# The last state-row blocks by half products, and four products in one bank

## The chip, the cores and the metric

The kernel runs on one core of a Trainium2 chip. The engines that the text speaks of are TensorE (PE; its weight loads are PEld), VectorE (DVE), ScalarE (ACT), GpSimd (POOL) and SyncE (SP), whose queue issues most of the DMAs. A time is the device time of one execution, in microseconds, and lower is better. The kernel before took 211.48, 212.24 and 214.16 us in three runs, median 212.24.

## The reference

Eight batches of attention between 512 tokens and 32 state rows, in both directions and in 8 heads of 64, are followed by a gated layer of width 1536. The 512 token rows and the 32 state rows of a batch go through the same layer.

```python
B, H, S, Ns, D = (8, 8, 512, 32, 64)
scores = scale * np.matmul(x, state.transpose(0, 1, 3, 2))
a = np.exp(scores - max);  a /= a.sum(-1)             # 512 x 32 in each head
xread = np.matmul(a, state)
scores2 = scale * np.matmul(state, x.transpose(0, 1, 3, 2))
a2 = softmax(scores2)
sread = np.matmul(a2, x)
attn_out = np.concatenate([xread, sread], axis=2)
x = attn_out.transpose(0, 2, 1, 3).reshape(B * S, H * D)   # 4352 rows of 512
gate = 1.0 / (1.0 + np.exp(-(x @ w_gate)))                 # 512 -> 1536
val = x @ w_val
return (gate * val @ w_out)                                # 1536 -> 512
```

## The kernel before, in words

**Token rows.** Since xread is a @ state, gate and value of a batch's token rows are a @ (state @ W). For each batch the kernel first forms SW = state @ W (32-row matmuls, `sw_mm`, line 286, and `sw_pair`, line 293, gate and value side by side), and then, for each of the twelve 128-wide blocks f of the 1536 columns, a gate half and a value half (`gv_half`, line 355): two matmuls of 512 columns each. ACT takes the tanh of the gate half (`gv_th`, line 364), DVE multiplies it with the value half into `glu` (`gv_glu`, line 369).

**Output product by seven half products.** glu @ w_out is cut in 2 x 2 blocks (two halves of the tokens; even and odd blocks f; two halves of the output columns) and done with seven products in the place of eight. The left operands are blocks of glu or sums of them (`s_sum`, line 414), the right ones blocks of w_out or sums of them. `w_mm(b, k, c)` (line 434) issues product k for one quarter of the tokens, six matmuls of 256 columns; "5a" in the table `order` is product 5, c = 0. Products that share a key add up in one PSUM bank. On the way the sums are read: V1 is product 1, U2 is 1 + 6, U4 is U2 + 5, and the four output blocks are V1 + 2, U2 + 5 + 3, U4 + 7 and U2 + 7 + 4. `w_keep` (ACT, line 439) copies a bank to SBUF, `w_add` (DVE, line 445) adds a bank to a kept tile, `w_out` (ACT, line 442) copies a bank to the output tile.

**Which products share a bank.** For the last two batches' outputs the table `CHAIN` holds: 1, 6, 5 and 3 follow each other in bank OU. For the others it is `KEY`: 1 and 6 share OU, then 5 and 3 start anew in OU, and DVE forms U4 and the last block by adding the kept U2.

**The order of the work** is written out by hand: each engine gets its instructions in the order in which the Python code names them, and works through them in that order. The main loop is `step(b, f)`, b = 2 to 7 and f = 0 to 11. A step of batch b does block f of gate and value of b, the products of `order[f]` for batch o = b - 1, and pieces of the preparation of batch nb = b + 1: two visits of state @ W (at f = 0 and f = 6, `sw_six`, three pairs of banks each), whose banks `sw_cp` (line 329, on ACT) copies out over the following steps, the scores (f = 1, 2) with their sums and reciprocals, and at f = 6 `rd_mm`, `rd_fin` (DVE, lines 273 and 275) and `rd_dma` (line 278): the state rows sread, normalised and transposed by a DMA on SP's queue into XS. SP's queue has the transposes of a, of XS and of x (lines 248, 278, 140) one behind the other. At f = 6 POOL also begins to cast the x of batch nb + 1 (lines 116 and 251).

**Banks.** There are eight, each with one tile at a time: G0 and G1 take gate and value halves, OU the products above, S0, S1, AT and the two of `X(b)` the rest. A tile is written only when every reader of the one before it in its bank is done.

**State rows.** The 256 state rows of all batches go through the layer at the end, as a ninth batch B. ACT reorders XS for this (line 1056), two columns at f = 9 and two at f = 10 of step 6. Blocks f = 0 to 7 of gate and value are computed by two groups of half products (`g_mm`, line 531, 128 x 128; g = 0 and 1, four blocks f each), woven into step(7, f) by the tables `g_main` and `g_side`. Their sums of weights (`g_wsum`, DVE, line 507) are spread over earlier steps by `g_early`. Like the products above, a group has a V1, U2 and U4 that ACT copies out (`g_keep`, line 540), DVE adds to (`g_add`, line 544), ACT takes the tanh of (`g_th`, lines 549 and 552) and DVE multiplies (`g_glu`, line 561). Blocks 8 to 11 are done directly after the loop by `last` (line 358, four matmuls of 256 columns for gate and for value). Then the output product of batch 7's tokens (`w_mm`, `p_mm`) and of the state rows (`q_mm`, line 571) ends the kernel.

## Time and profile before

| what | us |
|---|---|
| median of 3 runs (lowest, highest) | 212.24 (211.48, 214.16) |
| the profiled execution | 212.11 |
| its span, first to last instruction | 210.3 |
| TensorE busy | 202.2 |
| DVE busy | 168.5 |
| ACT busy | 135.0 |
| POOL busy | 79.4 |

The first 50 us of the span are loads and batches 0 and 1; steps of batch 2 to 7 run from 53 to 189, the tail from 189.3 on. Line numbers are those of the kernel before. In the views of the timeline a row gives the start, the time from the start to the end of the last of its instructions, the engine, the line, what is written and read, and in brackets how long the engine had been idle and what ended that. The recorded ends of matmuls are modelled, so in the chain of waits the time of a row is the time until the next one goes on.

### The profile page before, as it was taken

How to read it: one execution, taken by the hardware profiler on the slowest of the kernel's cores; microseconds unless marked ns; L12 is line 12 of the kernel's file. 1: busy time of each engine (PE TensorE's matmuls, PEld its weight loads, DVE VectorE, ACT ScalarE, POOL GpSimd, SP SyncE). 2: the span in 40 equal slices, each digit the busy share in tenths (PEclk: the TensorE clock that was granted, in tenths of full speed). 3: DMA queues.
4: the chain of work that ended last, by engine and by line, in shares of the span. 5: the costliest groups of instructions: out<-in, count | busy, mean ns of one | idle time of the engine just before them, and what ended most of it. 6: DMA issues, size and time to landing. Idle time of an engine off the chain costs nothing.

```text
span 210.3 us, 5452 instructions
## 1 busy us (share of the span) xinstructions
PE 202.2 (96%) x2137; PEld 132.1 (63%) x2137; DVE 168.5 (80%) x325; ACT 135.0 (64%) x254; POOL 79.4 (38%) x104
## 2 busy tenths in 40 slices
...
GB/s 198 178 192 192 213 288 189 120 203 52 78 208 343 131 100 64 311 118 136 298 95 67 155 101 16 44 102 202 12 47 0 203 2 3 0 97 100 7 151 148
DMA packets 40921, 27.15 MB, mean 129 GB/s; under 512 B 23616, under 2 KB 38720, under 8 KB 40896
## 3 DMA queue, kind: packets, MB, share of 16 engines
...
q10 hardware_dynamic: 432, 0.33, 0.5%
...
q14 instruction: 9, 0.07, 0.1%
...
## 4 chain that ended last, share of the span: by engine, by line
PE 91%; DMA 4%; POOL 2%; issue 1%; DVE 0%; POOLq 0%
PE gvp L355 30%; PE outp L434 29%; PE gvp L343 10%; DMA wgv<-in_moe_w_val_dram 4%; PE outp L454 4%; PE swp L286 4%; PE gvs L531 3%; PE outp L571 2%; PE swp L293 2%; PE gvp L358 2%; PE Sp L147 1%; PE outp L479 1%; POOL wgv L104 1%; PE rdp L262 1%; POOL xf L100 1%
## 5 line engine op out<-in xcount | busy, mean ns | idle before, releaser
L369 DVE SCALAR_TENSOR_TENSOR glu<-th,gvp 128x512 bf16<-128x512 f32 x96 | 64.9, 682 | 25.1 <-PE gvp L355 12.4
L364 ACT ACTIVATE th<-gvp 128x512 f32<-128x512 f32 (+1 forms) x100 | 59.1, 593 | 39.4 <-PE gvp L355 32.4
L355 PE MATMUL gvp<-aT,SW 128*128 128x512 bf16 x288 | 77.4, 379 | 0.0
L329 ACT CAST SW<-swp 128x512 bf16<-128x512 f32 x83 | 46.6, 591 | 9.5 <-PE swp L286 8.3
L434 PEld LDWEIGHTS <-Sm 128*128 128x128 bf16 x324 | 31.4, 98 | 11.0
L355 PEld LDWEIGHTS <-SW 128*128 128x128 bf16 x288 | 26.7, 98 | 17.0 <-issue 2.8
L200 POOL CAST Eb<-E 128x256 bf16<-128x256 f32 x32 | 13.7, 467 | 51.9 <-ACT E L167 51.9
L434 PE MATMUL outp<-tw,Sm 128*128 128x256 bf16 x240 | 31.6, 273 | 0.0
L434 PEld LDWEIGHTS <-glu 128*128 128x128 bf16 x240 | 23.3, 98 | 9.2
L434 PE MATMUL outp<-wo,glu 128*128 128x256 bf16 x168 | 22.7, 273 | 0.0
L343 PE MATMUL gvp<-aT,SW 128*128 128x512 bf16 x96 | 22.6, 379 | 0.0
L596 POOL DMA_DIRECT2D out_dram<-res x1 | 0.6, 612 | 50.4 <-ACT res L442 50.4
L227 POOL TENSOR_TENSOR ab<-E,ri 128x512 bf16<-128x512 f32 x13 | 14.3, 1101 | 10.9 <-DVE ri L210 6.3
L414 DVE TENSOR_TENSOR Sm<-glu 128x768 bf16<-128x768 bf16 x30 | 16.7, 558 | 0.0
L343 PEld LDWEIGHTS <-SW 128*128 128x128 bf16 x96 | 8.6, 98 | 10.5 <-issue 1.6
L445 DVE SCALAR_TENSOR_TENSOR res<-outp,U 128x512 f32<-128x512 f32 x20 | 13.6, 684 | 0.9 <-PE outp L454 0.9
L116 POOL CAST xb<-xf 128x1024 bf16<-128x1024 f32 x12 | 13.2, 1126 | 1.1 <-DMA xf<-in_x_dram 1.1
L167 ACT ACTIVATE E<-Sp 128x512 f32<-128x512 f32 x14 | 8.4, 598 | 7.1 <-PE Sp L147 5.7
L434 PE MATMUL outp<-wo,Sm 128*128 128x256 bf16 x84 | 11.3, 273 | 0.0
L251 POOL CAST xs<-xf 128x1024 bf16<-128x1024 f32 x10 | 10.2, 1043 | 0.0
L434 PE MATMUL outp<-tw,glu 128*128 128x256 bf16 x72 | 9.8, 273 | 0.0
L329 DVE CAST SW<-swp 128x512 bf16<-128x512 f32 x13 | 8.7, 684 | 1.2 <-PE swp L293 1.0
...
## 6 DMA issues: line engine op xcount, KB each, us to landing
...
```

The lines of the kernel that those rows point to most:

```text
L116: cp(xbs[b].rearrange("p c h d -> p h c d")[:, lo:lo + n], (xhs if b in xhs else xfs)[b][:, lo:lo + n])
L200: nc.gpsimd.tensor_copy(Ebs[b][:, c], E1s[b][:, c])
L227: (nc.gpsimd if eng is pool else nc.vector).tensor_tensor(half(b, i, abs_), e1, ri.unsqueeze(len(ri.shape)).to_broadcast(e1.shape), ALU.mult)
L251: pool(xs.rearrange("p c h d -> p h c d")[:, lo:lo + n, :, :D], xfs[b][:, lo:lo + n])
L329: cp(*sw_left.pop((b, lo, w, e)))
L343: nc.tensor.matmul(ps, SWs[b][:, g, w, fs], aTs[b][:, :, g], start=(g == 0), stop=(g == 1))
L355: nc.tensor.matmul(ps, SWs[b][:, g, w, fs], aTs[b][:, :, g], start=(g == 0), stop=(g == 1))
L364: nc.scalar.activation(th, held["gv", b, f][0], AF.Tanh, scale=0.5)
L369: nc.vector.scalar_tensor_tensor(glus[b][:, f], held["th", b, f], 1.0, held["gv", b, f][1], ALU.add, ALU.mult)
L414: eng.tensor_tensor(S_(b, t)[:, i], a, c, op)
L434: nc.tensor.matmul(wps[key][:, c], lhs[:, i, c * 128:(c + 1) * 128], rhs[:, i], start=(first and c == 0 and i == 0), stop=(i == NF // 2 - ...
L445: nc.vector.scalar_tensor_tensor(to, wps[key], 0.5, held["w", name], ALU.mult, ALU.add)
```

## The change

There are three edits. First, blocks 8 to 11 of the state rows become a third group, g = 2, of half products in banks S0, G1 and G0; `last` and its line 358 are gone, the weight sums of all groups move to other steps, with those of the third group in steps 6 and 7, and ACT's reorder of XS moves to f = 8 and 9 of step 6 (columns 0 and 1) and f = 0 of step 7 (columns 2 and 3). Second, `CHAIN` holds for every batch: 1, 6, 5 and 3 add up in OU from f = 0 to f = 10, ACT copies U4 out at f = 6 and the finished block at f = 10. For that 5b moves from f = 7 to f = 6 and 7a from f = 8 to f = 7. Third, the second visit of state @ W (f = 6) takes both gate/value banks in the place of one of them and OU, product 5a stands between this visit and the gate half, and which of G0 and G1 takes the gate changes with the batch and no longer at f = 6.

```diff
-    KEY = {1: 1, 6: 1, 2: 2, 5: 5, 3: 5, 7: 7, 4: 7}
     CHAIN = {1: 1, 6: 1, 5: 1, 3: 1, 2: 2, 7: 7, 4: 7}
 
     def w_mm(b, k, c):
 
         lhs, rhs = prod(b, k)
-        key = (CHAIN if b >= B - 2 else KEY)[k]
+        key = CHAIN[k]
         first = k == key
         if first and c == 0:
-            place = OU if key in (1, 5) else X(b)[key == 2]
...
@@ -523,7 +527,7 @@
         rhs = g_x(*{1: (0, 0), 2: (1, 0), 3: (1, 1)}[k]) if k < 4 else held["xt"][:, {4: 3, 5: 0, 6: 1, 7: 2}[k]]
         key = CHAIN[k]
         if k == key:
-            place = ((AT, S0, S0), (S1, AT, AT))[g][(1, 2, 7).index(k)]
+            place = ((AT, S0, S0), (S1, AT, AT), (S0, G1, G0))[g][(1, 2, 7).index(k)]
...
-    order = {0: "1a", 1: "1b", 2: "2a", 3: "2b", 4: "6a", 5: "6b", 6: "5a", 7: "5b", 8: "7a7b", 9: "3a", 10: "3b4a", 11: "4b"}
+    order = {0: "1a", 1: "1b", 2: "2a", 3: "2b", 4: "6a", 5: "6b", 6: "5a5b", 7: "7a", 8: "7b", 9: "3a", 10: "3b4a", 11: "4b"}
...
-    g_side = {0: ((g_xsum, 1), (s_sum, B - 2, 0, 1, nc.vector)),
+              8: ((1, 7),), 9: ((1, 5),), 10: ((1, 3),), 11: ((1, 4), (2, 1))}
+    g_side = {0: ((xs_order, 2), (xs_order, 3), (g_xsum, 1), (s_sum, B - 2, 0, 1, nc.vector)),
...
-              11: ((g_add, 1, 7, "U2"),)}
-
-    def sw_six(b, v):
+              11: ((g_add, 1, 7, "U2"), (g_keep, 2, "V1"))}
+
+    def sw_six(b, v, pair):
 
         if b not in SWs:
             SWs[b] = fp.tile((128, 2, 2, dff), BF, name="SW", bufs=2)
         lo = 768 * v
         x, y = X(b)
-        for k, places in enumerate((((x, G1), (S0, y), (OU, S1)) if v else ((OU, G0), (x, AT), (S0, S1)))):
...
@@ -970,16 +976,18 @@
 
         nb, o = (b + 1 if b + 1 < B else None), b - 1
         v, late = f // 6, 1 if b == 2 else 0
+        gb = ((G1, G0), (G0, G1))[b % 2 if nb else 0]
         if nb and f in (0, 6):
             if v:
                 rd_mm(nb, AT)
-            sw_six(nb, v)
+            sw_six(nb, v, gb)
             sw_cp(nb, v, 0, 1, act)
             sw_cp(nb, v, 2 * v, 0, act)
         todo = order[f]
-        gb = (G1, G0) if nb and not v else (G0, G1)
-
-        at = {0: 0, 6: 0, 10: 2, 11: 0}.get(f, len(todo)) if nb is not None else len(todo)
+        if nb and f == 6:
+            w_mm(o, 5, 0)
+            todo = todo[2:]
+        at = {0: 0, 10: 2, 11: 0}.get(f, len(todo)) if nb else len(todo)
...
         if f == 5 and nb:
             s_sum(o, 3, 1, nc.vector)
-        if f == 7:
-            if b == B - 1:
-                w_keep("U4", 1)
-            else:
-                held["w", "U4"] = fp.tile((128, 2, 256), FP, name="U4", bufs=1)
-                w_add(5, "U2", held["w", "U4"])
+        if f == 6:
+            w_keep("U4", 1)
...
         if f == 10:
-            if b == B - 1:
-                w_out(1, w_res(o, 0)[:, :, hi_])
-            else:
-                w_add(5, "U2", w_res(o, 0)[:, :, hi_])
+            w_out(1, w_res(o, 0)[:, :, hi_])
...
-        if b == B - 2 and f in (9, 10):
-            if f == 9:
-                held["XS"] = xp.tile((128, 4, B * Ns), BF, name="xb", padded_shape=(128, 4, H * D))
-            for j in (2 * f - 18, 2 * f - 17):
-                act(held["XS"][:, j].rearrange("p (n b) -> p n b", b=B), XS[:, :, j].rearrange("p b n -> p n b"))
+        if b == B - 2 and f in (8, 9):
+            xs_order(f - 8)
```

The tail, where `last(8)` to `last(11)` stood:

```diff
-    def last(f, *mid):
-        gv_half(B, f, 0, G0)
-        gv_th(B, f)
-        for k, c in mid:
-            w_mm(o, k, c)
-        gv_half(B, f, 1, (G1, S0)[f % 2])
-
-    last(8, (1, 0))
+    w_mm(o, 1, 0)
+    g_mm(2, 2)
     g_th(1, "U2")
-    gv_glu(B, 8)
     s_sum(o, 0, 1, nc.vector)
-    last(9, (1, 1), (2, 0))
+    g_add(2, 2, "V1")
+    g_mm(2, 6)
+    g_keep(2, "U2")
+    w_mm(o, 1, 1)
     w_keep("V1", 1)
-    gv_glu(B, 9)
+    g_th(2, "V1")
+    g_glu(1, "U2")
     s_sum(o, 1, 1, nc.vector)
-    g_glu(1, "U2")
-    last(10, (2, 1), (6, 0))
-    gv_glu(B, 10)
+    g_mm(2, 7)
+    g_mm(2, 5)
+    g_keep(2, "U4")
+    g_glu(2, "V1")
+    w_mm(o, 2, 0)
+    g_add(2, 7, "U4")
+    g_th(2, "U4")
+    w_mm(o, 2, 1)
     w_add(2, "V1", w_res(o, 0)[:, :, lo_])
     s_sum(o, 2, 1, nc.vector)
-    last(11, (6, 1))
+    g_mm(2, 3)
+    g_th(2, None)
+    g_glu(2, "U4")
...
+    w_mm(o, 6, 1)
     w_keep("U2", 1)
...
+    g_mm(2, 4)
+    g_add(2, 7, "U2")
+    g_th(2, "U2")
     p_mm(7, 0)
+    s_sum(o, 3, 0, nc.vector)
+    g_glu(2, "U2")
+    w_mm(o, 5, 0)
```

TensorE at step(6, 6), the first matmul of the visit's third pair and what follows, before (names: swp is the visit's bank, gvp a gate or value half, outp a bank of products):

```order
L293 LDWEIGHTS sTc_99
L293 MATMUL swp_2899<-wgv_101,sTc_99 32x512 [waits Activation_49]
...
L355 LDWEIGHTS SW_2280
L355 MATMUL gvp_2911<-aT_2545,SW_2280 128x512 [waits DVE_49]
...
L355 MATMUL gvp_2916<-aT_2545,SW_2280 128x512 [waits Activation_49]
...
L434 LDWEIGHTS Sm_104
L434 MATMUL outp_2919<-tw_103,Sm_104 128x256 [waits Activation_49]
```

And in the changed kernel:

```order
L293 LDWEIGHTS sTc_99
L293 MATMUL swp_2896<-wgv_101,sTc_99 32x512 [waits DVE_49]
...
L433 LDWEIGHTS Sm_104
L433 MATMUL outp_2705<-tw_103,Sm_104 128x256
...
L355 MATMUL gvp_2914<-aT_2550,SW_2278 128x512 [waits Activation_49]
...
L433 MATMUL outp_2705<-tw_103,Sm_104 128x256
...
L355 MATMUL gvp_2925<-aT_2550,SW_2278 128x512 [waits Activation_49]
```

The third pair's first matmul waits for DVE and no longer for ACT; 5a stands ahead of the gate half, and 5b ahead of the value half.

ACT from the tanh of f = 8 to that of f = 10 in step 6, before (th is a tanh, SW a cast of a visit's bank, COPY the reorder of XS):

```order
L364 ACTIVATE th_2961<-gvp_2958 128x512 [waits DVE_49,PE_49]
L329 CAST SW_2667<-swp_2900 128x2x256
L364 ACTIVATE th_2987<-gvp_2984 128x512 [waits DVE_49,PE_49]
L329 CAST SW_2667<-swp_2889 128x512
L1056 COPY xb_3001<-XS_105 128x256 [waits DMAHW4_49,DMAHW3_49,DMAHW5_49,DMAHW2_49,DMAHW6_49,DMAHW1_49,DMAHW7_49,DMAHW0_49,Pool_49]
L1056 COPY xb_3001<-XS_105 128x256
L364 ACTIVATE th_3007<-gvp_3004 128x512 [waits DVE_49,PE_49]
L1056 COPY xb_3001<-XS_105 128x256 x2
```

And in the changed kernel, where the last row is the copy of the finished block:

```order
L364 ACTIVATE th_2965<-gvp_2962 128x512 [waits DVE_49,PE_49]
L329 CAST SW_2664<-swp_2897 128x2x256
L511 COPY xb_2980<-XS_105 128x256 [waits DMAHW4_49,DMAHW5_49,DMAHW3_49,DMAHW6_49,DMAHW1_49,DMAHW7_49,DMAHW0_49,Pool_49]
L364 ACTIVATE th_2986<-gvp_2983 128x512 [waits DVE_49,PE_49]
L329 CAST SW_2664<-swp_2886 128x512
L511 COPY xb_2980<-XS_105 128x256
L364 ACTIVATE th_3004<-gvp_3001 128x512 [waits DVE_49,PE_49]
L441 ACTIVATE res_2822<-outp_2705 128x2x256 [waits PE_49]
```

The first copy, with its wait for the transposes, now stands ahead of the tanh of f = 9.

ACT in the tail, from the tanh of f = 11 of batch 7, before (E1 and xT hold the groups' V1, U2 and U4, gvs is a group's bank, V1 is the kept product of batch 7):

```order
L364 ACTIVATE th_3397<-gvp_3394 128x512 [waits PE_49,Activation_49]
L364 ACTIVATE th_3429<-gvp_3424 128x256 [waits DVE_49,PE_49]
L552 ACTIVATE E1_3236<-E1_3236 128x256 [waits DVE_49]
L364 ACTIVATE th_3451<-gvp_3446 128x256 [waits PE_49,Activation_49]
L439 ACTIVATE V1_3471<-outp_3431 128x512 [waits PE_49]
L364 ACTIVATE th_3481<-gvp_3476 128x256 [waits PE_49,Activation_49]
```

And in the changed kernel:

```order
L364 ACTIVATE th_3397<-gvp_3394 128x512 [waits PE_49,Activation_49]
L544 ACTIVATE E1_3427<-gvs_3407 128x512 [waits PE_49]
L556 ACTIVATE E1_3234<-E1_3234 128x256 [waits DVE_49]
L544 ACTIVATE E1_3427<-gvs_3407 128x512 [waits PE_49]
L438 ACTIVATE V1_3469<-outp_3435 128x512 [waits PE_49]
L556 ACTIVATE E1_3427<-E1_3427 128x256 [waits DVE_49]
L544 ACTIVATE xT_3167<-gvs_3407 128x512 [waits PE_49]
L556 ACTIVATE xT_3167<-xT_3167 128x256 [waits DVE_49]
```

The four tanhs of `last` are gone; three copies of bank gvs_3407, each ahead of or behind a tanh that waits for DVE, have come.

More of the change, by code (lines that the diff above doesn't have):

```diff
@@ L427, in w_mm @@
         lhs, rhs = prod(b, k)
-        key = (CHAIN if b >= B - 2 else KEY)[k]
+        key = CHAIN[k]
         first = k == key
         if first and c == 0:
-            place = OU if key in (1, 5) else X(b)[key == 2]
+            place = OU if key == 1 else X(b)[key == 2]
             wps[key] = place[0].tile((128, 2, 256), FP, name="outp", tag=place[1])
@@ L507, in g_wsum, with xs_order @@
         nc.vector.tensor_tensor(d, a, c, op)
+    def xs_order(j):
+        if j == 0:
+            held["XS"] = xp.tile((128, 4, B * Ns), BF, name="xb", padded_shape=(128, 4, H * D))
+        act(held["XS"][:, j].rearrange("p (n b) -> p n b", b=B), XS[:, :, j].rearrange("p b n -> p n b"))
     def g_x(k, h):
@@ L538, in g_keep @@
             gk["U4"] = ap_.tile((128, 2, 2, 2, 128), FP, name="xT")
-        t = held["g", g, name] = gk["U4"][:, g] if name == "U4" else gk[g][:, ("V1", "U2").index(name)]
+        t = held["g", g, name] = gk["U4"][:, g % 2] if name == "U4" else gk[g][:, ("V1", "U2").index(name)]
         nc.scalar.activation(t, gps_[g, 1], AF.Copy)
@@ L924 @@
     rd_fin(2)
-    order = {0: "1a", 1: "1b", 2: "2a", 3: "2b", 4: "6a", 5: "6b", 6: "5a", 7: "5b", 8: "7a7b", 9: "3a", 10: "3b4a", 11: "4b"}
+    order = {0: "1a", 1: "1b", 2: "2a", 3: "2b", 4: "6a", 5: "6b", 6: "5a5b", 7: "7a", 8: "7b", 9: "3a", 10: "3b4a", 11: "4b"}
     gate, val = slice(0, 1), slice(1, 2)
-    g_early = {(4, 6): ((0, 0),), (4, 7): ((0, 1, gate),), (4, 8): ((0, 1, val),), (5, 1): ((0, 2),), (5, 6): ((0, 3),),
-               (5, 7): ((1, 0, gate),), (5, 8): ((1, 0, val),), (6, 1): ((1, 1),), (6, 6): ((1, 2),), (6, 7): ((1, 3, gate),), (6, 8): ((1, 3, val),)}
+    g_early = {(4, 1): ((0, 0),), (4, 6): ((0, 1),), (4, 7): ((0, 2, gate),), (4, 8): ((0, 2, val),),
+               (5, 1): ((0, 3),), (5, 6): ((1, 0),), (5, 7): ((1, 1, gate),), (5, 8): ((1, 1, val),),
+               (6, 1): ((1, 2),), (6, 6): ((1, 3),), (6, 7): ((2, 0, gate),), (6, 8): ((2, 0, val),),
+               (7, 3): ((2, 1),), (7, 8): ((2, 2),), (7, 9): ((2, 3),)}
     g_main = {1: ((0, 1), (0, 2)), 2: ((0, 6),), 3: ((0, 7), (0, 5)), 4: ((0, 3),), 5: ((0, 4), (1, 1)), 6: ((1, 2),), 7: ((1, 6),),
-              8: ((1, 7),), 9: ((1, 5),), 10: ((1, 3),), 11: ((1, 4),)}
-    g_side = {0: ((g_xsum, 1), (s_sum, B - 2, 0, 1, nc.vector)),
+              8: ((1, 7),), 9: ((1, 5),), 10: ((1, 3),), 11: ((1, 4), (2, 1))}
+    g_side = {0: ((xs_order, 2), (xs_order, 3), (g_xsum, 1), (s_sum, B - 2, 0, 1, nc.vector)),
               1: ((g_keep, 0, "V1"), (g_add, 0, 2, "V1"), (g_xsum, 2)),
@@ L949, in sw_six @@
         x, y = X(b)
-        for k, places in enumerate((((x, G1), (S0, y), (OU, S1)) if v else ((OU, G0), (x, AT), (S0, S1)))):
+        for k, places in enumerate((((x, pair[0]), (S0, y), (pair[1], S1)) if v else ((OU, pair[1]), (x, AT), (S0, S1)))):
             pss = [p[0].tile((128, 512), FP, name="swp", tag=p[1]) for p in places]
```

5 lines of the change are left out of this document (2 added, 3 removed).

## The prediction

> **What bounds the kernel now.** I read the page's busy times first, then the waits of TensorE, then the busy times by stretch, one stretch for each batch of the steady part (97.33 to 119.45 is batch 4) and one for the tail (189.30 to 199.40).
>
> ```profile
> PE 202.2 (96%) x2137; PEld 132.1 (63%) x2137; DVE 168.5 (80%) x325; ACT 135.0 (64%) x254; POOL 79.4 (38%) x104
> ...
> PE swp L293 <- DMA wgv<-in_moe_w_val_dram: 1.1, 2, 0.7
> ...
> 97.33:119.45 22.12, 22.12 (x237) 14.12 (x244) 18.55 (x35) 15.11 (x28) 8.08 (x10) 1.00 0.53 142
> ...
> 189.30:199.40 10.10, 10.10 (x100) 9.06 (x99) 8.40 (x21) 3.66 (x8) 0.00 (x0) 1.00 0.15 56
> ```
>
> In both stretches TensorE is busy for the whole length (22.12 of 22.12, 10.10 of 10.10) at a granted clock of 1.00. The waits of TensorE are six rows, all at the kernel's start like the one shown; the same view cut to 50 to 206 us lists none. So for 155 us the time is the sum of the matmuls issued. An edit can gain only what it takes off that sum, and it can lose wherever it lets TensorE meet a bank or an operand that isn't ready. DVE and ACT work that comes or goes counts only through such a meeting.
>
> **Part 1: the last eight state-row visits (f = 8 to 11 of gate and value) become a third group of half products.** The chain of waits gives the pace at which matmuls follow each other.
>
> ```profile
> 174.39 0.89 PE gvs L531 x16
> ...
> 192.74 0.87 PE gvp L358 x8
> ```
>
> Removed: 32 matmuls of line 358, 4 x 0.87 = 3.48 us. Added: 7 products of 8, 56 matmuls of line 531, 3.5 x 0.89 = 3.12 us. **Term: -0.37 us**, all of it on the bound engine. [...]
>
> **Part 2: products 1, 6, 5 and 3 in one bank.** Per batch DVE loses two evictions (line 445) and ACT gains two; TensorE issues the same matmuls. OU is now held from f = 0 to f = 10, so the second state @ W visit of step f = 6 must use another pair: both gate/value banks. Here is that step in batch 6.
>
> ```profile
> 151.43 0.59 PE L355 MATMUL gvp<-aT,SW 128*128 128x512 bf16 x2
> ...
> 152.12 1.74 ACT L329 CAST SW<-swp 128x512 bf16<-128x512 f32 x3
> 152.13 0.69 DVE L369 SCALAR_TENSOR_TENSOR glu<-th,gvp 128x512 bf16<-128x512 f32 x1 [0.23 <-PE gvp L355]
> ...
> 152.75 0.41 PE L293 MATMUL swp<-wgv,sTc 64*32 64x512 bf16 x8
> ...
> 153.09 1.04 PE L355 MATMUL gvp<-aT,SW 128*128 128x512 bf16 x4
> ```
>
> The value half of f = 5 starts at 151.43; its glu ends at 152.82, 1.39 later. The third pair of the visit (line 293) starts at 152.75, 1.32 after the value half. Before, it went to OU and S1; now its first matmul goes to the value bank of f = 5 and needs that glu. What a release costs, TensorE's early waits show:
>
> ```profile
> 7.33 0.42 DVE L135 COPY xT<-xTp 128x512 bf16<-128x512 bf16 x1 [0.16 <-PE xTp L132]
> ...
> 7.82 0.29 PE L174 MATMUL Sp<-tw,xT 128*128 128x64 bf16 x4 [0.29 <-DVE xT L135]
> ```
>
> DVE ends at 7.75, TensorE goes on at 7.82: 0.06. So the pair comes 1.39 + 0.06 - 1.32 = 0.13 late, in each of batches 2 to 6, with the whole PE queue behind it. **Term: 5 x 0.13 = +0.65** (0.35 to 1.0, as a release takes nothing or twice that). Nothing covers it. The gate half of f = 6 also needs a cast now (the second of the three in the ACT row, over at about 153.3), but 5a stands ahead of it: visit end 153.09, 5a about 0.77 with the change of tile shape, so it comes at 153.9. That edit I cost at nothing; without 5a it would wait 0.3.
>
> **Part 3: what the new order of f = 6 to 8 does.** 5a and 5b now stand ahead of the value half of f = 6, which starts at 153.09 + 0.77 + 0.43 + 0.66 = 154.95 instead of 153.63, 1.3 later, and the next steps are 2 x 0.43 + 0.66 = 1.52 long. The pace of hand-over to ACT and DVE is in three rows of step 8 and 9:
>
> ```profile
> 157.88 1.03 PE L355 MATMUL gvp<-aT,SW 128*128 128x512 bf16 x4
> 158.58 0.69 DVE L369 SCALAR_TENSOR_TENSOR glu<-th,gvp 128x512 bf16<-128x512 f32 x1 [0.55 <-PE gvp L355]
> ...
> 158.94 0.60 ACT L364 ACTIVATE th<-gvp 128x512 f32<-128x512 f32 x1 [1.10 <-PE gvp L355]
> ```
>
> A value half is followed 0.70 later by its glu, a gate half (here at 158.31) 0.63 later by its tanh. The value bank is thus free 1.39 + 0.06 = 1.45 after its start, against a step of 1.52: DVE may come 0.07 late before TensorE waits. In batch 2 it comes later, since a reduce and a reciprocal stand between the two glus:
>
> ```profile
> 65.94 0.69 DVE L369 SCALAR_TENSOR_TENSOR glu<-th,gvp 128x512 bf16<-128x512 f32 x1 [1.11 <-ACT th L364]
> ...
> 67.94 0.69 DVE L369 SCALAR_TENSOR_TENSOR glu<-th,gvp 128x512 bf16<-128x512 f32 x1
> ```
>
> Glu 7 can start 2.00 after glu 6. With glu 6 at value half + 0.70, glu 7 ends at + 3.39 and its bank is free at + 3.45; value half 8 is due at 2 x 1.52 = + 3.04. **Term: +0.41 in batch 2** (0 to 0.5). In batches 4 to 6 a weight sum (line 507) stands there instead:
>
> ```profile
> 109.90 2.02 POOL L251 CAST xs<-xf 128x1024 bf16<-128x1024 f32 x2
> ...
> 111.17 1.29 DVE L507 TENSOR_TENSOR xf<-wgv 128x1024 bf16<-128x1024 bf16 x1
> ...
> 133.29 1.45 DVE L507 TENSOR_TENSOR xf<-wgv,xf 128x1024 bf16<-128x1024 bf16 x1
> ...
> 154.40 0.69 DVE L369 SCALAR_TENSOR_TENSOR glu<-th,gvp 128x512 bf16<-128x512 f32 x1 [1.11 <-ACT th L364]
> 155.41 0.68 DVE L507 TENSOR_TENSOR xf<-wgv 128x1024 bf16<-128x1024 bf16 x1
> ```
>
> It took 1.29 and 1.45 in batches 4 and 5, and 0.68 in batch 6, where POOL had no casts. Moved 1.25 us later, to about 112.4, it starts after the cast that ends at 111.92, so I take 0.68 in all three: glu 7 then starts 155.41 + 0.61 - 154.40 = 1.62 after glu 6, its bank is free at + 3.07, and **the term is 3 x 0.03 = +0.1** (0 to 2, the upper end with 1.29 and 1.45 again). [...]
>
> **Part 4: the reorder of XS, two columns a batch step earlier.** ACT's first copy moves from f = 9 to f = 8 of batch 6 and needs the last transpose of XS.
>
> ```profile
> 150.38 5.80 SPq L248 DMA_TRANSPOSE aT<-ab  x4
> ...
> 155.20 0.29 DVE L275 TENSOR_TENSOR xr<-rdp,rr 128x128 bf16<-128x128 f32 x1
> ...
> 156.27 1.18 SPq L278 DMA_TRANSPOSE XS<-xr  x1
> ...
> 159.90 1.20 ACT L1056 COPY xb<-XS 128x256 bf16<-128x256 bf16 x2
> ...
> DMA to landing us min/median/max: 2.3/2.3/2.3
> ```
>
> Today SP's queue sets that transpose (busy with aT to 156.18), and it lands at 158.6, well before 159.90. With glu 6 1.25 later, xr ends at about 156.75, the issue follows at 156.9, the landing at 159.2. ACT gets there at 158.6, after tanh 8 (gate half 8 at 156.90, tanh at 157.53, then one cast). It waits to 159.3, copies 0.66 and only then does tanh 9, which ends at 160.47; gate half 10 is due at 159.94 and needs it. Of 0.59 I take off what the batch already lost at value half 8 and round: **term +0.45** (0 to 0.7). At the start of batch 7 the two other copies stand behind tanh 0 and end just as product 2 of group 0 wants them; nothing, up to 0.1.
>
> **Part 5: the tail's own chain.** Group 2 needs bank S0 three times, each time emptied by ACT, behind tanhs that wait for DVE.
>
> ```profile
> 183.94 0.59 ACT L540 ACTIVATE xT<-gvs 128x512 f32<-128x512 f32 x1
> ...
> 188.87 0.59 PE L355 MATMUL gvp<-aT,SW 128*128 128x512 bf16 x2
> ...
> 189.57 0.69 DVE L369 SCALAR_TENSOR_TENSOR glu<-th,gvp 128x512 bf16<-128x512 f32 x1
> 190.18 0.68 DVE L544 SCALAR_TENSOR_TENSOR E<-gvs,E 128x512 f32<-128x512 f32 x1
> 190.78 0.68 DVE L445 SCALAR_TENSOR_TENSOR res<-outp,U 128x512 f32<-128x512 f32 x1
> 191.38 0.55 DVE L414 TENSOR_TENSOR Sm<-glu 128x768 bf16<-128x768 bf16 x1
> 191.84 0.41 DVE L369 SCALAR_TENSOR_TENSOR SW<-th,gvp 128x256 bf16<-128x256 f32 x1
> ...
> 190.90 0.42 ACT L552 ACTIVATE E<-E 128x256 f32<-128x256 f32 x1 [0.57 <-DVE E L544]
> ```
>
> Product 1 of group 2 puts the last value half at 188.87 + 0.45 = 189.32, its glu at 190.02. Ahead of the sum that V1's tanh needs, DVE has three evictions at 0.60 and two state sums at 0.46: start 192.75, end 193.43; the tanh 0.04 later, the eviction of U4 0.33 behind it and 0.59 long: 194.39, with the release 194.45. TensorE reaches product 3 after 0.43 + 4 x 0.66 + 4 x 0.45 = 4.85 from 189.32, at 194.17. **Term: +0.3** (0 to 0.6). The four added weight sums in batches 6 and 7 fall where DVE waits for TensorE anyway (0.68 each, no POOL work there), at nothing; if they ran late, this chain would move with them.
>
> **The sum.** -0.37 + 0.65 + 0.41 + 0.1 + 0.45 + 0.3 = +1.54. The profiled execution took 212.11 (span 210.3 and 1.8 around it), 0.13 under the median of 212.24 and inside 211.48 to 214.16. 212.11 + 1.54 = **213.6**, 0.7% slower, inside the 2% (4.2 us) that a measurement of this kernel can tell from no change.
>
> **Rivals.** (a) The covers hold: releases and landings come early enough, and only the saving is left: 212.11 - 0.37 = 211.7. For it speaks that each wait above is under 0.6 us and three hang on 0.1; against it, that the third pair's wait follows from two rows alike in every batch. Chance 0.27. (b) The weight sum at f = 6 still meets POOL's casts, at 1.29 and 1.45 instead of 0.68 in batches 4 and 5, and at as much in batch 6 if POOL runs late there: glu 7, and so value half 8, comes another 0.6 to 0.77 late, three times, +2.1: 215.7, slower. It decides when POOL's last cast ends after glu 6 + 1.0; today's margin is 112.4 - 111.9. Chance 0.09. (c) Batch 2's later reduce moves POOL's casts and SP's transposes for batch 4:
>
> ```profile
> 72.56 5.15 SPq L140 DMA_TRANSPOSE xT<-xb  x4
> ...
> 80.72 0.40 PE L147 MATMUL Sp<-sTz,xT 128*128 128x64 bf16 x8
> ```
>
> 1.25 later they issue to 78.96 and land, like XS above, about 1.1 after the issue: 80.1, wanted at 80.5. If that fails, the loss is at most the shift less that margin, 213.6 + 0.9 = 214.5. Chance 0.04. (d) The weight load, and not the streaming, sets the pace of the half products once they are most of the tail:
>
> ```profile
> L531 PEld LDWEIGHTS <-xf 128*128 128x128 bf16 x64 | 4.2, 98 | 1.7
> ```
>
> 56 loads of 98 ns are 5.49 us in the place of 3.12: 213.6 + 2.4 = 216.0. Against it, the chain has 16 pairs in 0.89 us: loads run under the matmul before them. Chance 0.01. [...] That the change doesn't do what it says is excluded by the order of its instructions.
>
> **The numbers.** Forecast 0.58, (a) 0.27, (b) 0.09, (c) 0.04, (d) 0.01; 0.01 is left for a gain I don't see, since nothing but the 0.37 lies on the bound engine. The range is 211.4 to 215.3: from (a) less the half of its scatter to the forecast with its upper bounds, leaving out most of (b). Slower by over 2% (216.5) needs (b) and every other upper bound: 0.04. Faster by over 2%: 0.01. Within 2%: 0.95.
>
> **What would show it.** Right: a wait of TensorE at line 293 on DVE of about 0.1 in five batches; value half 8 of batch 2 late by 0.4; ACT idle at f = 8 of batch 6 on XS; product 3 of group 2 waiting for ACT; the weight sums of f = 6 at 0.7. Wrong: no such rows and a steady period still at 22.1 us, (a); sums at 1.3 and over, (b); line 531 above 60 ns a pair, (d).

## The result, and the profile after

The changed kernel takes 214.25 us (median of 6, 213.82 to 216.26) where the kernel before takes 212.16 (median of 6, 211.44 to 214.16): ratio 1.0111, 95% interval 1.0070 to 1.0153. It is about 1.1% slower, which is within the 2%. (A ratio is worked out from all runs of both kernels but those in a slower state of the chip, not from the medians, so the two can differ a little.) The forecast was 213.6, the range 211.4 to 215.3. Its profiled execution took 213.82, with a span of 212.0.

From the page of the changed kernel, the busy times and the engines' shares of the chain of waits; ahead of them, the chain's row of the page of before:

```profile
PE 91%; DMA 4%; POOL 2%; issue 1%; DVE 0%; POOLq 0%
```

```profile
PE 204.2 (96%) x2161; PEld 133.0 (63%) x2161; DVE 164.6 (78%) x322; ACT 141.9 (67%) x267; POOL 80.2 (38%) x104
...
PE 81%; DVE 5%; issue 4%; POOL 3%; ACT 2%; DMA 2%; SPq 2%; POOLq 0%; DVEq 0%; ACTq 0%
```

TensorE is busy for 96% of the span, as before, and yet the chain runs through it for 81% instead of 91%: there are now places where TensorE waits and another engine carries the chain. The view of TensorE's waits from 50 us on has two rows (us in total, times, longest), where before had none:

```profile
PE Sp L147 <- DMA xT<-xb: 0.4, 1, 0.4
PE gvp L355 <- ACT th L364: 0.4, 1, 0.4
```

To find the rest I cut both traces at the visits. A column is the time from the first matmul of one state @ W visit (line 286) to that of the next, from the visit at f = 6 of batch 2 on; the last column runs from the visit at f = 6 of batch 6 to the start of the tail's last product (line 479, in the changed kernel 478).

| kernel | 2: f 6-12 | 3: f 0-6 | 3: f 6-12 | 4: f 0-6 | 4: f 6-12 | 5: f 0-6 | 5: f 6-12 | 6: f 0-6 | 6: to the end | sum |
|---|---|---|---|---|---|---|---|---|---|---|
| before | 11.30 | 10.81 | 11.31 | 10.81 | 11.30 | 10.81 | 11.31 | 10.81 | 53.38 | 141.84 |
| changed | 11.73 | 11.35 | 11.71 | 10.81 | 11.43 | 10.82 | 11.44 | 10.81 | 53.92 | 144.02 |
| changed, second trace | 11.74 | 11.41 | 11.70 | 10.81 | 11.44 | 10.81 | 11.44 | 10.81 | 53.92 | 144.08 |

The sums differ by 2.18 and 2.24, the medians by 2.09. (The first visit of the table starts between 63.37 and 64.25 in the traces of all kernels here, at 63.85 in that of before and at 63.39 in that of the changed one; what lies ahead of it differs as much between executions as between kernels, and is left out here.) The steady stretches repeat to 0.01, so each difference can be looked up in the timeline. These are the places, in the changed kernel.

The visit of batch 6, timeline:

```profile
152.61 0.59 PE L355 MATMUL gvp<-aT,SW 128*128 128x512 bf16 x2
153.31 0.69 DVE L369 SCALAR_TENSOR_TENSOR glu<-th,gvp 128x512 bf16<-128x512 f32 x1 [0.23 <-PE gvp L355]
153.49 0.62 PE L286 MATMUL swp<-wgv,sTc 64*32 64x512 bf16 x16
154.06 0.41 PE L293 MATMUL swp<-wgv,sTc 64*32 64x512 bf16 x8
```

The same visit starts in before with this row; its third pair, at 152.75, stands in the prediction:

```profile
152.31 0.62 PE L286 MATMUL swp<-wgv,sTc 64*32 64x512 bf16 x16
```

The third pair starts 0.57 behind the visit's start; before it was 152.75 - 152.31 = 0.44. That is 0.13, and it is the same in batches 2 to 6. The view of the waits has no row for it, since the ends of matmuls are modelled; it is read from the starts.

The value half of f = 8, in batch 2 and in batch 3 (the row of four matmuls is the value half of f = 7 and the gate half of f = 8):

```profile
66.75 0.69 DVE L369 SCALAR_TENSOR_TENSOR glu<-th,gvp 128x512 bf16<-128x512 f32 x1 [2.38 <-ACT SW L329]
67.36 0.68 DVE L208 TENSOR_REDUCE rs<-E 128x16 f32<-128x512 f32 x1
...
68.66 0.68 DVE L369 SCALAR_TENSOR_TENSOR glu<-th,gvp 128x512 bf16<-128x512 f32 x1
69.39 1.02 PE L355 MATMUL gvp<-aT,SW 128*128 128x512 bf16 x4
...
90.64 1.03 PE L355 MATMUL gvp<-aT,SW 128*128 128x512 bf16 x4
...
91.71 0.69 DVE L369 SCALAR_TENSOR_TENSOR glu<-th,gvp 128x512 bf16<-128x512 f32 x1 [0.79 <-PE gvp L355]
92.45 1.02 PE L355 MATMUL gvp<-aT,SW 128*128 128x512 bf16 x4
```

In batch 2, glu 7 stands behind the reduce, and value half 8 comes 0.30 late. In batch 3 there is no reduce, DVE is idle for 0.79, and still glu 7 comes 1.07 behind its value half instead of 0.70; value half 8 is 0.27 to 0.29 late. Nothing in the prediction spoke of that.

Batch 3's second S product and the transposes of xT it needs; the last row is from the view of the tile xT from 70 to 85 us, and in before it reads 2.5/2.5/2.5:

```profile
77.26 1.27 SPq L140 DMA_TRANSPOSE xT<-xb  x1
80.69 0.28 PE L147 MATMUL Sp<-sTz,xT 128*128 128x64 bf16 x4
81.34 0.29 PE L147 MATMUL Sp<-sTz,xT 128*128 128x64 bf16 x4 [0.37 <-DMA xT<-xb]
```

```profile
DMA to landing us min/median/max: 2.5/2.5/4.0
```

Half of the product's eight matmuls wait for the last transpose, which took 4.0 from issue to landing (77.26 to 81.3): 0.54 us.

The reorder of XS in batch 6, and the third product of group 2 in the tail:

```profile
160.47 0.64 ACT L511 COPY xb<-XS 128x256 bf16<-128x256 bf16 x1 [0.66 <-issue]
161.01 0.59 ACT L364 ACTIVATE th<-gvp 128x512 f32<-128x512 f32 x1
161.66 0.59 PE L355 MATMUL gvp<-aT,SW 128*128 128x512 bf16 x2 [0.35 <-ACT th L364]
...
194.67 1.47 PE L433 MATMUL outp<-wo,glu 128*128 128x256 bf16 x12
195.30 0.42 ACT L556 ACTIVATE E<-E 128x256 f32<-128x256 f32 x1 [0.73 <-DVE E L548]
195.63 0.58 ACT L544 ACTIVATE xT<-gvs 128x512 f32<-128x512 f32 x1
196.26 0.61 PE L535 MATMUL gvs<-xb,xf 128*128 128x128 bf16 x8
```

ACT waits for XS, whose last transpose lands at 160.25 (the profile names no releaser for that row, but the copy's instruction waits for the transposes); tanh 9 follows, and gate half 10 comes 0.51 late. Product 3 comes 0.27 late, behind the copy of U4: the twelve matmuls ahead of it start at 194.67 and take 1.31, to 195.98, and it starts at 196.26. (The expectations below take 0.52 and 0.29 for these two.) Together: 5 x 0.13 + 0.30 + 0.54 + 0.28 + 0.51 + 0.27 - 0.37 = 2.18.

### The profile page after: what moved, and what is told of

It is laid out like the page before. It is cut to its first block, busy times and chain, and to the rows that moved or that the text cites. A ratio compares the mean times of both kernels' runs of the same rounds, so it can differ in the third digit from the quotient of the medians.

```text
span 212.0 us, 5503 instructions
## 1 busy us (share of the span) xinstructions
PE 204.2 (96%) x2161; PEld 133.0 (63%) x2161; DVE 164.6 (78%) x322; ACT 141.9 (67%) x267; POOL 80.2 (38%) x104
## 4 chain that ended last, share of the span: by engine, by line
PE 81%; DVE 5%; issue 4%; POOL 3%; ACT 2%; DMA 2%; SPq 2%; POOLq 0%; DVEq 0%; ACTq 0%
PE gvp L355 25%; PE outp L433 23%; PE gvp L343 10%; PE outp L453 4%; PE gvs L535 4%; PE swp L286 3%; PE swp L293 2%; PE outp L575 2%; DMA xT<-xb 2%; PE warm L608 2%; SPq L140 2%; DVE glu L369 1%; PE Sp L147 1%; PE outp L478 1%; POOL xs L251 1%
## 5 line engine op out<-in xcount | busy, mean ns | idle before, releaser
L364 ACT ACTIVATE th<-gvp 128x512 f32<-128x512 f32 x96 | 57.4, 602 | 29.8 <-PE gvp L355 27.1
L433 PEld LDWEIGHTS <-Sm 128*128 128x128 bf16 x324 | 30.9, 98 | 12.0 <-issue 1.1
L433 PE MATMUL outp<-tw,Sm 128*128 128x256 bf16 x240 | 32.3, 273 | 0.0
L444 DVE SCALAR_TENSOR_TENSOR res<-outp,U 128x512 f32<-128x512 f32 x15 | 10.2, 685 | 0.9 <-PE outp L453 0.9
L438 ACT ACTIVATE U<-outp 128x512 f32<-128x512 f32 x15 | 9.1, 604 | 1.9 <-PE outp L433 1.2
```

The lines of the kernel that those rows point to most:

```text
L364: nc.scalar.activation(th, held["gv", b, f][0], AF.Tanh, scale=0.5)
L433: nc.tensor.matmul(wps[key][:, c], lhs[:, i, c * 128:(c + 1) * 128], rhs[:, i], start=(first and c == 0 and i == 0), stop=(i == NF // 2 - ...
L444: nc.vector.scalar_tensor_tensor(to, wps[key], 0.5, held["w", name], ALU.mult, ALU.add)
```

## The experiments

Theory: these waits, and nothing else, are the loss, and each is on the path. Rivals: the loss sits in the tail (part 1), the odd delays in batches 2 and 3 are accidents of one execution, or a wait taken away only uncovers the next. The first four kernels ran on the same chip.

**The changed kernel again.**

> The changed kernel itself, on the same chip as the other three. Theory: ratio 1.009 to 1.012; its trace has the third pair 0.57 behind the visit's start in five batches, value half 8 of batch 2 and of batch 3 each 0.3 late, and the second half of S in batch 3 waiting for xT. If the waits in batches 2 and 3 were accidents of one execution, the last three rows are missing here and the ratio is 1.006 or less.

214.41 against 212.13, ratio 1.0128 (1.0084 to 1.0172). The ratio is just above the expected 1.012. The table's third row is its trace: every delay is back, to within 0.06. They are no accidents.

**Part 1 alone.** The kernel before, with the tail, the weight sums, the XS copies and batch 7 of the changed kernel:

```
-    last(8, (1, 0))
+    w_mm(o, 1, 0)
+    g_mm(2, 2)
...
-        gb = (G1, G0) if nb and not v else (G0, G1)
+        gb = (G1, G0) if not nb or not v else (G0, G1)
```

> The kernel before with part 1 alone: group 2 by half products in the tail, with its weight sums, the earlier reorder of XS, and in batch 7 alone the new order of products and banks. Batches 2 to 6 keep the old bank for products 5 and 3 and the old visit. Theory (the waits add up): the tail exchange -0.37, product 3 of group 2 late by 0.3. The reorder of XS should cost little here, since glu 6 of batch 6 is not late and xr ends 1.3 us earlier than in the changed kernel: 0 to 0.2 instead of 0.52. Sum 0.0 to +0.15 us, ratio 1.000 to 1.001. Rival (the tail carries the loss: 128-column pairs cost more than the few rows show, or the added weight sums of batches 6 and 7 delay the tail): +1 us or more, ratio 1.005 or more, and a tail longer than before's from the last main value half on.

212.46 against 212.13, ratio 1.0017 (0.9994 to 1.0040). The stretches up to batch 6 are those of before, the last is 53.89: +0.51, so the rival with 1 us or more is out, but I had expected 0.15 at most. From the visit on, 0.11 is lost at XS, then 0.51 at the start of batch 7, then 0.27 at product 3. The 0.51 is of my making: here batch 6 ends on one order of the two gate/value banks and batch 7 begins on the other.

**Parts 2 and 3 alone.** The changed kernel with the tail, batch 7, weight sums and XS copies of before.

> The changed kernel without part 1: the tail, batch 7, the weight sums and the reorder of XS are those of before; batches 2 to 6 keep one bank for products 1, 6, 5 and 3 and the visit in both gate/value banks. Theory: 5 x 0.13 at the third pair, 0.30 at value half 8 of batch 2, 0.54 at the second half of batch 3's S product behind the transposes of xT, and 0.29 at value half 8 of batch 3 if that is no accident of one execution: 0.65 + 0.30 + 0.54 + 0.29 = +1.8 us, ratio 1.008. Rival (it lies in the tail): 0 to +0.5, ratio 1.000 to 1.002. Rival (the batch 2 and 3 delays were an accident of one execution): +0.65 to +0.95 us, ratio 1.003 to 1.0045, and no wait on xT in its trace.

216.15 against 212.13, ratio 1.0183 (1.0150 to 1.0216): +4.0, twice the expectation and more than the whole change. Up to batch 5 its stretches are those of the changed kernel (11.74, 11.31, 11.71, 10.81, 11.44, 10.81, 11.43). Then come 11.08 for 10.81, and 54.38 at the end, 1.00 over before. Its timeline at f = 9 to 11 of batch 6:

```profile
161.61 1.20 ACT L1056 COPY xb<-XS 128x256 bf16<-128x256 bf16 x2
162.69 0.61 ACT L364 ACTIVATE th<-gvp 128x512 f32<-128x512 f32 x1
163.18 0.61 ACT L441 ACTIVATE res<-outp 128x512 f32<-128x512 f32 x1
163.66 1.18 ACT L1056 COPY xb<-XS 128x256 bf16<-128x256 bf16 x2
164.57 0.82 PE L433 MATMUL outp<-tw,glu 128*128 128x256 bf16 x6
164.72 0.62 ACT L364 ACTIVATE th<-gvp 128x512 f32<-128x512 f32 x1
165.37 0.69 DVE L369 SCALAR_TENSOR_TENSOR glu<-th,gvp 128x512 bf16<-128x512 f32 x1 [0.88 <-ACT th L364]
166.11 0.59 PE L355 MATMUL gvp<-aT,SW 128*128 128x512 bf16 x2 [0.72 <-DVE glu L369]
```

Part 2 puts the eviction of the finished block (line 441) on ACT at f = 10, where before had four XS copies: tanh 11 is late, its glu is late, and TensorE, through with product 4 at 164.57 + 0.66 = 165.23, goes on at 166.11: 0.88. So the earlier reorder, which costs 0.51 in the changed kernel, also makes room for part 2; the parts don't add up. This profiled execution is 3.93 longer than that of before (216.04 against 212.11). Its stretches have 2.87 of that, and the places account for all of it: 5 x 0.13 at the third pair, 0.30 in batch 2, 0.50 at xT and 0.27 at glu 7 in batch 3, 0.27 in the stretch of 11.08 (it is told below) and 0.88. Its start is 0.29 earlier, and the other 1.35 lies behind the last product, 0.66 in the span and 0.69 outside. I have no cause for that part.

**Four covers put back.**

```
-    def sw_six(b, v, pair):
+    def sw_six(b, v, pair, mid):
...
+            if v and k == 2:
+                mid()
...
-            sw_six(nb, v, gb)
+            sw_six(nb, v, gb, lambda: w_mm(o, 5, 0))
...
-            w_mm(o, 5, 0)
...
-                if f == ((2, 3), (3, 6))[late][i]:
+                if f == ((2, 3), (3, 5))[late][i]:
                     n_sum(nb, i)
-                if f == ((2, 3), (4, 6))[late][i]:
+                if f == ((2, 3), (4, 5))[late][i]:
                     n_mul(nb, i, pool)
...
-        if b == B - 2 and f in (8, 9):
-            xs_order(f - 8)
+        if b == B - 2 and f in (9, 10):
+            xs_order(f - 9)
...
+    w_mm(o, 6, 0)
     g_mm(2, 3)
...
-    w_mm(o, 6, 0)
     w_mm(o, 6, 1)
```

> The changed kernel with four covers put back: the first product 5a stands ahead of the visit's third pair; the second reduce and multiply of batch 3's attention run a step earlier in batch 2; XS is reordered at f = 9 and 10 of batch 6 again; half of product 6 stands ahead of product 3 of group 2. Same work, same banks. Theory (each wait is on the path): 0.65 + 0.30 + 0.54 + 0.52 + 0.29 = 2.3 us off the changed kernel, so 0.0 to -0.3 against before, ratio 0.9985 to 1.000; the trace has no wait of line 293 on the glu, none on xT, none of gate half 10 on the XS copy and none of product 3 in the tail. Rival (another wait is right behind each one): less than half of it comes back, ratio above 1.005.

213.31 against 212.13, ratio 1.0054 (1.0034 to 1.0074): about half came back, and the expected 1.000 at most was missed. Its stretches are 11.53, 10.81, 11.82, 10.81, 11.53, 10.81, 11.54, 10.81, 53.36. The waits at xT, XS and product 3 and the one of batch 2 are gone, but each f 6-12 still has 0.23 too much (batch 3 has its 0.28 besides). The visit of batch 5:

```profile
130.81 0.63 PE L286 MATMUL swp<-wgv,sTc 64*32 64x512 bf16 x16
131.37 0.83 PE L433 MATMUL outp<-tw,Sm 128*128 128x256 bf16 x6
...
132.13 0.41 PE L293 MATMUL swp<-wgv,sTc 64*32 64x512 bf16 x8
132.47 0.60 PE L355 MATMUL gvp<-aT,SW 128*128 128x512 bf16 x2
```

5a waits for no one, yet it starts 0.56 behind the visit's start where two pairs take 0.44, and the third pair starts 0.76 behind it where six matmuls take 0.66. The cover is of tile shape 128*128 between matmuls of 64*32, and the two turns cost 0.12 and 0.10: more than the 0.13 it hid.

**Three covers, without that one.**

> The changed kernel with three of the four covers of the earlier kernel: batch 2's reduce a step earlier, XS at f = 9 and 10, half of product 6 ahead of product 3 of group 2. Product 5a stands behind the visit's third pair again. Theory (the cover at the visit cost more than the wait: it changed the tile shape twice, 0.12 ahead of 5a and 0.10 behind it, for a wait of 0.13): the twelve steps from the visit of f = 6 to the next visit take 11.44 in batches 2, 4, 5 and 6 instead of 11.53, five times -0.09 = -0.45 us, so 0.7 us over before, ratio 1.003 to 1.004. Rival (5a ahead of the third pair did pay, and the rest of the loss is elsewhere): 1.2 us over before or more, ratio 1.0055 or more.

212.53 against 211.99, ratio 1.0009 (0.9985 to 1.0032); stretches 11.42, 10.81, 11.71, 10.81, 11.43, 10.81, 11.44, 10.81, 53.25, in sum 0.65 over before, as expected (0.7); the ratio came out below the expected 1.003, which its interval holds. So the cover at the visit did cost 0.09 each time, and the three others bring back 0.30, 0.54 to 0.60 and 0.67. The 0.67 is 0.11 less than 0.51 + 0.27: something in the tail takes back a part (the last section of the experiments finds it at product 4).

**The bank wanted earlier.** Is it really the glu that the third pair waits for? The second and the third pair exchange banks and data.

```
-        for k, places in enumerate((((x, pair[0]), (S0, y), (pair[1], S1)) if v else ((OU, pair[1]), (x, AT), (S0, S1)))):
+        for k, places in enumerate((((x, pair[0]), (pair[1], S1), (S0, y)) if v else ((OU, pair[1]), (x, AT), (S0, S1)))):
...
-            sw_cp(nb, v, 2 * v, 0, act)
+            sw_cp(nb, v, v, 0, act)
...
```

> The changed kernel with the visit's second and third pair exchanged, banks and data: the value bank of f = 5 is now wanted 0.22 earlier, by the second pair. Same work. Theory (TensorE waits for the glu to empty that bank): the second pair still starts 0.57 behind the visit's start, the wait is 0.35 instead of 0.13, and the twelve steps take 0.22 longer in each of batches 2 to 6, 11.66 instead of 11.44; +1.1 us over the changed kernel, ratio to before 1.015 to 1.018. Rival (the 0.13 belongs to the third pair's own form, not to the bank): no change, 11.44, ratio 1.011.

215.57 against 212.16, ratio 1.0179 (1.0141 to 1.0217); f 6-12 takes 11.65 and 11.66 in batches 4 and 5, 0.22 more, as expected (in batches 2 and 3, which have their other delays, 11.95 and 11.92). The visit of batch 6:

```profile
153.49 0.59 PE L355 MATMUL gvp<-aT,SW 128*128 128x512 bf16 x2
...
154.37 0.41 PE L286 MATMUL swp<-wgv,sTc 64*32 64x512 bf16 x8
154.93 0.41 PE L286 MATMUL swp<-wgv,sTc 64*32 64x512 bf16 x8 [0.15 <-DVE glu L369]
```

Now the profile names the glu, and the pair that needs the bank comes 1.44 behind the value half (153.49), as the third pair did (152.61 to 154.06: 1.45). The time at which the bank comes free is fixed by the value half, whichever pair asks for it.

**One more DVE instruction ahead of the odd glu, and two more matmuls in the warm-up.** For the delay in batch 3 without a visible cause.

```
                 rd_fin(nb)
+                if b == 3:
+                    nc.vector.reciprocal(ap_.tile((128, 2, 1), FP, name="rr"), held["rd", nb][:, :, D:])
```

```
     zero(sbz, pool)
-    warm(4, S1)
+    warm(6, S1)
```

> The changed kernel with one more instruction on DVE: a second reciprocal of the row sums, 0.16 us, between xr and glu 7 of batch 3, its result not used. In three traces of the changed queue glu 7 of batch 3 came 1.07 behind its value half instead of 0.70, at the instant of tanh 8, with DVE idle. Theory (an accident of where DVE stands in its stream of instructions): glu 7 comes at 0.70 to 0.72 and the steps from the visit on take 11.44 instead of 11.71 in batch 3. Rival (TensorE reports the value half late there): still 1.07, and 11.70.

> The changed kernel with two more matmuls in the warm-up ahead of the first transposes, so that every later instruction of TensorE stands four places further on in its stream, and nothing else is changed. Theory (an accident of DVE's stream): glu 7 of batch 3 still 1.07 behind its value half, 11.70 from the visit on. Rival (an accident of TensorE's stream): the delay is gone from batch 3, or stands at another place.

Each ran once (215.08 and 214.81 us), so only the traces are read. With DVE's stream moved by one, batch 3's glu comes 0.71 behind its value half and the stretch takes 11.43; with TensorE's moved by four rows, 1.06 and 11.70. Timeline of the first, batch 3:

```profile
91.65 1.03 PE L355 MATMUL gvp<-aT,SW 128*128 128x512 bf16 x4
...
91.84 0.16 DVE L1048 RECIPROCAL rr<-rdp 128x2 f32<-128x2 f32 x1
92.36 0.69 DVE L369 SCALAR_TENSOR_TENSOR glu<-th,gvp 128x512 bf16<-128x512 f32 x1 [0.35 <-ACT SW L329]
```

The delay was not gone, though: it came back in batch 6, where 6: f 0-6 took 11.08, as it did with parts 2 and 3 alone. There, glu 3 comes 1.05 behind its value half:

```profile
150.29 1.03 PE L355 MATMUL gvp<-aT,SW 128*128 128x512 bf16 x4
...
151.34 0.69 DVE L369 SCALAR_TENSOR_TENSOR glu<-th,gvp 128x512 bf16<-128x512 f32 x1 [0.23 <-PE gvp L355]
```

I counted DVE's stream from its start, with the separate wait instructions. The late glu of batch 3 is number 192 in all eight traces that have it, the late glu of batch 6 number 320 in both that have it; in the traces without the delay, no glu of these batches has a multiple of 64. So it is tied to the place in DVE's stream. A multiple of 64 alone doesn't make a glu late, though. In part 1 alone and its three later versions number 256 is a glu of batch 4 that waits for TensorE too, and it comes 0.70 behind its value half. Number 384, in batch 7 of the run with the added reciprocal, comes 0.71 behind. From part 1 alone:

```profile
116.35 0.59 PE L355 MATMUL gvp<-aT,SW 128*128 128x512 bf16 x2
...
117.05 0.69 DVE L369 SCALAR_TENSOR_TENSOR glu<-th,gvp 128x512 bf16<-128x512 f32 x1 [0.35 <-PE gvp L355]
```

What happens at 192 and 320, and not at 256 and 384, is open.

**Eighty more rows in TensorE's stream.** In five traces of the changed order one packet of a queue that the profile calls instruction fell into the time in which the last xT transpose was under way. Its row from the view of the DMA queues, from 79.2 to 79.6 us (packets, MB, share of 16 engines):

```profile
q8 instruction: 1, 0.02, 16.0%
```

It starts at 79.24, and the transpose lands 1.0 behind its end. In before such a packet starts at 79.40, when the last xT transpose, issued at 76.44, is through (78.92). There it falls on the next transpose in the queue, one of XS, issued at 77.75 and not wanted at once, which takes 4.1. From the view of before's tile XS, 77 to 82 us:

```profile
DMA to landing us min/median/max: 2.4/3.3/4.1
```

Forty matmuls of 8 columns in the warm-up move the packet:

```
     warm(3, G0)
+    ps = G0[0].tile((128, 512), FP, name="warm", tag=G0[1])
+    for _ in range(40):
+        nc.tensor.matmul(ps[:, :8], wm, wm[:, :8], start=True, stop=True)
```

> The changed kernel with 40 tiny matmuls (8 columns, result not used) in the warm-up, 80 more rows in TensorE's stream. In the five traces of the changed queue the last transpose of xT in batch 2 landed 4.0 to 4.4 after its issue instead of 2.5, and in each of them one packet of the instruction queue, 16 KB, started 1.9 to 2.2 after that issue. Theory (the transpose waited behind the instruction packet): the packet comes about 3 us earlier against the visit, the transpose lands 2.5 after its issue and S_mm of batch 3 does not wait: 10.81 from visit to visit. Rival (the packet has nothing to do with it): it lands 4.0 or later again, and the stretch takes 11.3 or more. The total is longer by the added matmuls and says nothing.

The kernel ran once (214.17). The packet comes at 76.2, 4 us earlier against the visit, and the stretch takes 10.81: the S product no longer waits, though casts and transposes stand where they stood.

```profile
80.38 3.78 SPq L278 DMA_TRANSPOSE XS<-xr  x3
81.55 0.40 PE L147 MATMUL Sp<-sTz,xT 128*128 128x64 bf16 x8
```

```profile
DMA to landing us min/median/max: 2.5/2.9/4.2
```

One of the four still takes 4.2: the first, issued at 74.23, which is under way when the packet comes and which nobody wants at once. So the last transpose was late because of the packet. In the two runs of the section before this one the last transpose took 4.36 and 4.40, and the stretch 11.67 and 11.71.

**Part 1 alone, mended.** What is the exchange worth by itself? First with before's XS copies and half of product 6 ahead of product 3; then with batch 7 on before's banks and the sum S3 ahead of two later sums; then with the evictions of the tail in another order:

```
-        gb = (G1, G0) if not nb or not v else (G0, G1)
+        gb = (G1, G0) if nb and not v else (G0, G1)
...
-    for part in range(3):
+    for part in (1, 0, 2):
         p_add("U4", part, 1)
```

> The kernel before with part 1 alone, its two waits taken away: XS is reordered where before had it (two copies at f = 9, two at f = 10 of batch 6, ACT has no eviction of products 5 and 3 there), and half of product 6 stands ahead of product 3 of group 2. Theory: of part 1 alone, +0.51 in its trace from the visit of batch 6 on, the wait at XS (0.12 + 0.34) and that at product 3 (0.28) go; what stays is the exchange, -0.25 to -0.37: ratio 0.9982 to 0.9990, faster than both kernels. Rival (the tail's chain waits at another place once product 3 comes later): 0.0 to +0.3 us, ratio 1.000 to 1.0015, with a wait behind product 4 or the last sums.

211.94 against 211.99, ratio 0.9987 (0.9968 to 1.0007), last stretch 53.63: XS and product 3 no longer wait, but the 0.51 at the swapped banks stayed. The expectation missed that; that the ratio came out in its range is luck, since the stretch is 0.25 longer than before's.

> Part 1 alone, with the two waits of the earlier version of it taken away: batch 7 keeps before's gate and value banks (that version swapped them, and gate half 0 then met four XS copies and a bank that glu 11 had to empty, 0.51 late), group 2's banks are swapped to fit, and the sum S3 of the state rows' last products stands ahead of two later sums on DVE, where 0.12 was given back. Theory: only the exchange is left, 0.37 less from the visit of batch 6 to the last product, 53.0 instead of 53.38: ratio 0.998, faster than both kernels. Rival (another wait of the tail takes its place): 53.25 or more, ratio 0.9995 or more.

211.69 against 212.16, ratio 0.9982 (0.9959 to 1.0006), last stretch 53.13. The 0.51 is gone. At the tail's first `p_mm` the saving is exactly 0.37, at the end 0.25: moving S3 was the wrong mend for the 0.12.

> The last version of part 1 alone, with DVE's three evictions of the tail's U4 parts in the order 1, 0, 2 instead of 0, 1, 2. In that version the exchange stood at -0.37 up to the first p_mm of the tail and at -0.25 at the end: product 4 of part 1 came 0.12 later behind product 3 than in before, at the time at which DVE was through with parts 0 and 1. Theory (product 4 waited for the eviction of part 1, behind that of part 0): the 0.12 comes back, 53.0 from the visit of batch 6 to the last product, ratio 0.9975 to 0.998, faster than before. Rival (the 0.12 is something else): 53.13 again, ratio 0.998 to 0.9985.

211.55 against 212.06, ratio 0.9966 (0.9941 to 0.9991), last stretch 53.01: 0.37 less than before. Product 4 did wait for the eviction of part 1, which had stood behind that of part 0. It started 0.67 behind the first of the three evictions in the version ahead of this one (the first two rows), and starts 0.54 behind it now:

```profile
200.76 0.81 DVE L485 SCALAR_TENSOR_TENSOR res<-outp,U 128x256 f32<-128x256 f32 x3
201.43 0.49 PE L479 MATMUL outp<-tw,glu 128*128 128x128 bf16 x6
...
200.52 0.81 DVE L485 SCALAR_TENSOR_TENSOR res<-outp,U 128x128 f32<-128x128 f32 x3
201.06 0.50 PE L479 MATMUL outp<-tw,glu 128*128 128x128 bf16 x6
```

This version, the kernel before with part 1 and without parts 2 and 3, is faster than both: by 0.37 us, 0.2%, in the trace, and the interval of its ratio lies below 1. That is far within the 2%, and the ratio's 0.3% is more than the trace accounts for. Its chain from 150 us on holds nothing but TensorE up to the last two evictions.

## Why the prediction was right or wrong

The verdict (within 2%, a little slower) and the range were right; the sum, +1.54, was short of the 2.2 that the traces show. Two terms of 0.8 in all were missing from it, and the time fell inside the range only because upper bounds had been set for other terms: that much was luck. Term by term:

- **Part 1, -0.37:** right to the hundredth. It takes a tail without waits to see it (53.01 against 53.38). The half products ran at the pace of the row that the prediction took, so its rival (d) is out: 16 pairs take 0.89 us in the trace of the last version too, 56 ns each.
- **Part 2, 5 x 0.13:** right in size, place and cause; the exchanged pairs show that the wait is the bank's. (The row of line 293 on DVE that was to show it is not in the view of the waits.)
- **Part 3, batch 2, 0.41:** 0.30. glu 7 started 1.91 behind glu 6 (66.75 to 68.66), not 2.00. (The value half of f = 6 starts at 153.53 in before, not at 153.63, and 5a takes 0.66, not 0.77; these two cancel.)
- **Part 3, weight sums, 0.1:** about 0. They took 0.68 and 0.69, as taken, so rival (b) did not come (in batches 4 and 5 they start at 113.36 and 135.61, with POOL's last casts over at 112.93 and 135.25; in before they ran beside those casts, at 1.29 and 1.45), and the 0.03 that each was to cost did not show.
- **Part 4, 0.45:** 0.51. The step was as told: xr, issue, landing, copy, tanh, gate half. What the earlier reorder is good for was not told: without it part 2's eviction would have cost 0.88 there.
- **Part 5, 0.3:** 0.27, though a mend of it brings back 0.12 less, since product 4 then waits for an eviction.

Two things were missing. **Rival (c)**, at a chance of 0.04, came. Batch 2's later reduce moved the transposes by 1.27 against the visit of f = 6 (the first was issued 8.71 behind it before, 9.98 now), which is the 1.25 that was taken. The step that failed is the landing: it was taken as about 1.1 behind the end of the issue, as one transpose of XS had it, and it came 2.8 behind (issued to 78.53, landed at 81.29), which made S_mm 0.54 to 0.60 late. A landing has a tail, and the trace of before shows it: its XS transpose issued at 77.75 took 4.1. There the last xT transpose was through 0.5 ahead of the packet. The margin of 0.4 at S_mm was read as safe on the landing of a single transpose. The second is **0.27 in batch 3**, which no row of before could give: it depends on where the change leaves an instruction in DVE's stream, and its cause is open.

Rival (a), the covers hold, had 0.27; it was right for the weight sums alone and wrong at the other four places. That three terms hung on margins of 0.1 was a reason for it in the prediction; the rows repeat to 0.01, so a margin of 0.1 was enough to decide.
